# Sigmoid attention and SwiGLU on one core: two more quads transposed by DMA, halves of a tile written by two engines, a later first visit, last stores by rows

## The chip, the core and the metric

The kernel runs on one core of a Trainium2 chip. The core has engines that run side by side, each with its own queue of instructions: TensorE (PE, matmuls; PEld is its weight load), VectorE (DVE), ScalarE (ACT), GpSimd (POOL) and SyncE (SP). Data moves between the chip's memory (HBM), the on-chip SBUF and, on the core, the matmul accumulator PSUM. Transfers are issued from the queues of SP, ACT and POOL and carried out by the core's 16 DMA engines. The metric is the device time of one execution in microseconds (us); lower is better.

## The reference

```python
scores = q @ k.transpose(0, 1, 3, 2) / sqrt(64) - log(448)     # 8 batches, 12 heads, 448 x 64
attn_out = sigmoid(scores) @ v                                 # no softmax: a plain sigmoid
x = attn_out.transpose(0, 2, 1, 3).reshape(3584, 768)
g = x @ w_gate                                                 # 768 x 1536
out = (g * sigmoid(g) * (x @ w_val)) @ w_out                   # 1536 x 768, float32
```

## The kernel before

The attention works in **quads**: four heads of one batch, three quads per batch, 24 in all (quad n belongs to batch n // 3). One quad goes through these steps:

- `load` (L129) brings q and k as float32 into a staging tile `st` (448 KB each); `load_v` (L134) brings v as float16.
- `cast` (L139) makes a bf16 tile `c16` of it, on VectorE for the first quads, on GpSimd (L145) for the later ones.
- The bf16 tile is transposed into `T` (pool `qkT`, four buffers for q and four for k). `trans_pe` (L159) does it on TensorE: 14 matmuls against an identity (L167) into PSUM and two copies out of it on VectorE (L175). `trans_dma` (L150) does it by two DMA transposes issued on SyncE (L153), one for q and one for k.
- `qk_tile` (L185) makes the scores of one seventh of the keys (4 matmuls, L191), `sig_tile` (L200) takes the sigmoid on ScalarE (L202), and `pv` (L205) multiplies with v once all seven are there (28 matmuls, L214). The result is copied out of PSUM into two tiles `xT` of 128 partitions, each in two halves of 64 (L228 on VectorE). For quad 2, with `two=True`, ScalarE copies the second halves (L226).

The feed-forward part uses `xT` as its right-hand side. `ffn1` (L246) computes one of 12 feature tiles f of one batch: 12 matmuls (L239), a sigmoid on ScalarE (L253) and two multiplications on VectorE (L255, L259) that write `hT`. `ffn2` (L265) computes one of 7 output tiles for a pair of batches: 24 matmuls (L273), an eviction in two halves on VectorE (L307) and two stores of 64 rows each (L318). For the very last tile the second half is evicted by ScalarE (L293, 192 columns) and VectorE (L300, 192 columns), and each half is stored by two transfers, one from SyncE and one from ScalarE (L315).

All PSUM users take turns on a ring of four buffers `D0` to `D3`, two banks each (`Banked`, L75). The framework tracks which instruction reads and writes which tile and adds the waits; `add_to_no_dep_group` and `declare_no_dep` take a wait away where the program knows that there is no conflict.

The order of the work is written out by hand. The prologue (L361 to L434) handles quads 0 to 2 and the first two feature tiles of batch 0. Then a loop (L465) walks over `units`, the feature and output tiles with planned times of 2.26 and 3.9 us. Into it it inserts **visits** (L339): each quad from 3 on has two, the first with four of its score tiles, the second with three. A visit is due when the planned time `tcur` has reached its `vtime` (L340 to L348). For the quads of batch 1 (3, 4, 5) these due times are spread evenly between `2 * FU1` and `FIRST`.

The tables `begin` (L449 to L459) say what GpSimd and SyncE are given after a visit: `ready(n)` (L441) casts quad n and, for n >= `NPE`, issues its DMA transposes; `fetch(n)` (L436) loads quad n; `w_load` (L113) loads a quarter of w_gate, w_val or w_out (576 KB as float16). `NPE = 2 * NJ = 6`, so quads 4 and 5 are transposed on TensorE: `post` (L476, L486) calls `trans_pe` one unit behind the second visit of the quad before. GpSimd's queue is in program order: a fetch stands behind the casts that were issued ahead of it, and a cast waits for its load to land.

Of the kernel before, what the change touches and what calls it, by code (L numbers as in the profile page):

```python
# [9 lines left out]
FP32 = mybir.dt.float32  # L10
# [3 lines left out]
MULT = mybir.AluOpType.mult  # L14
# [3 lines left out]
def kernel(  # L18
# [10 lines left out]
    nc = tc.nc  # L29
    ctx.enter_context(tc.manual_schedule())  # L30

    B, H, S, D = q.shape
    DM = H * D
    DFF = moe_w_gate.shape[1]
    C = S // D
    NJ = H // 4
# [5 lines left out]
    HREC = 1.0 / HSC  # L42
# [86 lines left out]
    def load(n, which, eng=None):  # L129
        st = stg.tile([128, 2, S], FP32, tag="stg", name=f"st{which}_{n}")  # L130
        (eng or nc.sync).dma_start(out=st, in_=src_of(n, which))  # L131
        qkv_st[(n, which)] = st

    def load_v(n):  # L134
        t = v16p.tile([128, 2, S], FP16, tag="v16", name=f"v16_{n}")
        nc.gpsimd.dma_start(out=t, in_=src_of(n, 2))  # L136
        v16[n] = t

    def cast(n, which, eng, lo=0, hi=C):  # L139
        st = qkv_st[(n, which)]  # L140
        if hi == C:
            qkv_st.pop((n, which))
        t = c16.tile([128, hi - lo, 2, D], BF16, tag="c16" if hi - lo == C else f"c16_{lo}", name=f"c16_{which}_{n}")
        q16[(n, which, lo)] = t
        eng.tensor_copy(  # L145
            out=t.rearrange("p c h d -> p h c d"),
            in_=st.rearrange("p h (c d) -> p h c d", c=C)[:, :, lo:hi, :],
        )

    def trans_dma(n, which):  # L150
        t = q16.pop((n, which, 0))
        d = qkT.tile([128, C, 128], BF16, tag=f"T{which}", name=f"T{which}_{n}")
        nc.sync.dma_start_transpose(out=d, in_=t.rearrange("p c h d -> p (c h d)"))  # L153
        for c in range(C):
            qT[(n, which, c)] = d[:, c]
        if which == 0:
            qT[(n, 0)] = d

    def trans_pe(n, parts=((0, 0, C), (1, 0, C))):  # L159

        D2 = Banked()
        ps = D2.t.bitcast(BF16).rearrange("p w (c i) -> p w c i", c=8)
        for i, (which, lo, hi) in enumerate(parts):
            t = q16.pop((n, which, lo))
            for c in range(hi - lo):
                D2.write(
                    nc.tensor.transpose(  # L167
                        out=ps[:, i, c, :], in_=t[:, c].rearrange("p h d -> p (h d)"), identity=idn
                    ),
                    i,  # L170
                )
        for i, (which, lo, hi) in enumerate(parts):
            tag = f"T{which}" if hi - lo == C else f"T{which}_{lo}"
            d = qkT.tile([128, hi - lo, 128], BF16, tag=tag, bufs=None if hi - lo == C else 1, name=f"T{which}_{n}_{lo}")
            D2.read(nc.vector.tensor_copy(out=d, in_=ps[:, i, :hi - lo, :]), i)  # L175
            for c in range(lo, hi):
                qT[(n, which, c)] = d[:, c - lo]
            if which == 0:
                qT[(n, 0)] = d
# [25 lines left out]
    def pv(n, two=False):  # L205
        b, j = divmod(n, NJ)
        P = Banked().t
        vt = v16.pop(n)
        for c in range(C):
            pt = pts.pop((n, c))  # L210
            for h2 in range(2):
                for w in range(2):
                    r = slice(w * 64, w * 64 + 64)
                    nc.tensor.matmul(  # L214
                        out=P[h2 * 64:(h2 + 1) * 64, w, :S],
                        lhsT=vt[r, h2, c * D:(c + 1) * D],
                        rhs=pt[r, h2, :],
                        start=(c == 0),
                        stop=(c == C - 1),
                    )  # L220
        for h2 in range(2):
            x = xtp.tile([128, S], FP16, tag="xT", name=f"xT_{b}_{2 * j + h2}")
            for w in range(2):
                o, i = x[w * 64:(w + 1) * 64, :], P[h2 * 64:(h2 + 1) * 64, w, :S]
                if two and w == 1:
                    nc.scalar.copy(out=o, in_=i)  # L226
                else:
                    nc.vector.tensor_copy(out=o, in_=i)  # L228
            xT[(b, 2 * j + h2)] = x


# [33 lines left out]
    def ffn2(pb, m):  # L265
        hw = DM // 2
        osb = osp.tile([128, DM], FP32, tag="osb", name="osb")
        D = Banked("o")
        for half in range(2):
            for f in range(NF):  # L270
                h = hT[(pb, f)].rearrange("p b s -> p (b s)")
                D.write(
                    nc.tensor.matmul(  # L273
                        out=D.t[:, half, :hw],
                        lhsT=h[:, m * 128:(m + 1) * 128],
                        rhs=wo16[f // FW][:, f % FW, half * hw:(half + 1) * hw],
                        start=(f == 0),
                        stop=(f == NF - 1),
                    ),
                    half,  # L280
                )
        last = pb == B // 2 - 1
        dsts = []
        for i in range(2):
            bb, c = divmod(2 * m + i, C)
            bb += 2 * pb
            dsts.append(out[bb * S:(bb + 1) * S, :].rearrange("(p c) n -> c p n", c=C)[c])
        for half in range(2):
            hs = slice(half * hw, (half + 1) * hw)
            if last and m == C - 1 and half == 1:  # L290
                qw = hw // 2
                D.read(
                    nc.scalar.activation(  # L293
                        out=osb[:, hw:hw + qw], in_=D.t[:, 1, :qw],
                        func=mybir.ActivationFunctionType.Copy, scale=HREC,
                    ),
                    1,
                )
                D.read(
                    nc.vector.tensor_scalar(  # L300
                        out=osb[:, hw + qw:], in0=D.t[:, 1, qw:hw], scalar1=HREC, scalar2=None, op0=MULT
                    ),
                    1,
                )
            else:
                D.read(
                    nc.vector.tensor_scalar(  # L307
                        out=osb[:, hs], in0=D.t[:, half, :hw], scalar1=HREC, scalar2=None, op0=MULT
                    ),
                    half,  # L310
                )
            if last and m == C - 1:
                for i in range(2):
                    eng = nc.sync if i == 0 else nc.scalar
                    eng.dma_start(out=dsts[i][:, hs], in_=osb[i * 64:(i + 1) * 64, hs])  # L315
        if not (last and m == C - 1):
            for i in range(2):
                (nc.sync if last else nc.gpsimd).dma_start(out=dsts[i], in_=osb[i * 64:(i + 1) * 64, :])  # L318


    FU1, FU2 = 2.26, 3.9
# [18 lines left out]
    vtime = []  # L340
    for grp in visits:
        n, c = grp[0]
        b, j = divmod(n, NJ)
        frac = (j * C + c) / (NJ * C)
        if b == 1:
            vtime.append(2 * FU1 + frac * (FIRST - 2 * FU1))
        else:
            vtime.append(FIRST + 1.0 + (b - 2 + frac) * PER)  # L348

# [5 lines left out]
            for n, c, sc in scs:  # L355
                sig_tile(n, c, sc)

    NPE = 2 * NJ


    V, G = nc.vector, nc.gpsimd  # L361
# [7 lines left out]
    cast(0, 1, V, 0, 2)  # L369
    trans_pe(0, ((0, 0, C), (1, 0, 2)))  # L370
    cast(0, 1, V, 2, C)

    def chunk(n, c):
        sig_tile(n, c, qk_tile(n, c))
# [39 lines left out]
    pv(1)  # L414
    chunk(2, 3)
    trans_pe(3)
    cast(4, 0, G)
    cast(4, 1, G)
    w_load("v", 2)
    load_v(5)  # L420
    w_load("g", 3)
# [11 lines left out]
        ffn1_mm(Df, 0, f, range(NP - 2, NP))  # L433
        ffn1_gate(Df, 0, f)  # L434

    def fetch(n):  # L436
        load(n, 0, G)
        load(n, 1, G)
        load_v(n)

    def ready(n):  # L441
        cast(n, 0, G)
        cast(n, 1, G)
        if n >= NPE:
            trans_dma(n, 0)
            trans_dma(n, 1)


    begin = {(n, i): [] for n in range(NJ, NQ) for i in range(2)}  # L449
    begin[(4, 0)] += [lambda: ready(5), lambda: fetch(6)]  # L450
# [10 lines left out]

    tcur = 2 * FU1
    vi = 0
    pend, post = [], []
    for dur, fn, args in units:  # L465
        while vi < len(visits) and tcur >= vtime[vi]:
            group = visits[vi]
            vi += 1
            pvs, pend = pend, []
            attn_step(group, pvs)  # L470
            n, c = group[-1]
            for act in begin[(n, int(c == C - 1))]:
                act()
            if c == C - 1:
                pend.append(n)
                if n + 1 < NPE:  # L476
                    post.append(n + 1)
        if pend and (
            fn is ffn1 and args[1] == 0 and (args[0], NP - 1) not in xT
            or vi == len(visits) and tcur >= vtime[-1] + 4.0  # L480
        ):
            for n in pend:
                pv(n)
            pend = []
        fn(*args)
        while post:  # L486
            trans_pe(post.pop())
        tcur += dur


# [28 lines left out]
```

## Time and profile before

| what | value |
|---|---|
| median of 11 runs | 442.28 us (439.11 to 443.74) |
| profiled execution | 440.32 us, of which the span of its instructions is 438.5 us |
| granted TensorE clock in it, mean | 0.992 |
| TensorE transposes L167 | 14 matmuls in 0.94 us per quad |
| ffn1 matmuls L239 | 1152 of about 353 ns |
| ffn2 matmuls L273 | 672 of 326 ns |
| loads issued by GpSimd, median to landing | q 5.2, k 8.7, v 9.5, w_gate 14.5, w_val 15.0, w_out 17.2 us |
| DMA transposes, 36 of them, median to landing | 6.1 us |

The page's busy time per engine is a share of the whole span. Its DMA row cuts the span into 40 slices of about 11 us, each digit being the busy tenths of the 16 DMA engines. q0 is the queue of transfers that GpSimd issues, q1 that of SyncE. "To landing" is the time from issue to the last byte, and so holds the time that a transfer waits behind others.

### The profile page before, as it was taken

The numbers are of one execution on the slowest core, as the hardware profiler recorded it, in microseconds if no ns is written. First come the engines' busy times: TensorE is split into PE (matmuls) and PEld (weight loads), VectorE is DVE, ScalarE is ACT, GpSimd is POOL, SyncE is SP. The second block draws the span as 40 slices with busy tenths as digits, with TensorE's granted clock in tenths as the row PEclk, the third lists the DMA queues.
The fourth block names the chain that finished last, engine by engine and source line by source line (L and its number), as shares of the span: only waits on it lengthen the run. The fifth ranks groups of instructions, "written<-read, shape, count | busy, mean of one in ns | idle before, by whom it ended". The sixth has DMA issues, their size and how long they took to land.

```text
span 438.5 us, 7904 instructions
## 1 busy us (share of the span) xinstructions
PE 417.3 (95%) x3261; PEld 219.5 (50%) x3261; DVE 220.2 (50%) x364; ACT 207.7 (47%) x269; POOL 116.1 (26%) x166
## 2 busy tenths in 40 slices
PE   6788779999999999999999999999999999999995
PEld 3434345445555445445555545444555545555563
DVE  3644646465344457556434456647524356555331
ACT  4967557546433555645533655745623452222000
POOL 4464434042255546000245534400012200000000
PEclk8999989999999999999999999999999999999999
DMA  8999999999598998600198999820022400000144
GB/s 303 237 269 205 244 165 187 148 114 183 116 136 196 253 216 157 134 1 1 29 137 192 219 150 216 197 43 1 0 73 73 100 9 1 1 1 1 42 103 108
DMA packets 57796, 54.38 MB, mean 124 GB/s; under 512 B 35680, under 2 KB 52448, under 8 KB 57760
## 3 DMA queue, kind: packets, MB, share of 16 engines
q0 software_dynamic: 20896, 39.20, 43.4%
q1 hardware_dynamic: 36432, 14.03, 20.9%
q10 hardware_dynamic: 432, 0.66, 0.4%
q8 instruction: 25, 0.41, 0.4%
q14 instruction: 11, 0.09, 0.1%
HBM read 47.19 MB, written 11.01 MB: 133 GB/s over the span
## 4 chain that ended last, share of the span: by engine, by line
PE 82%; ACT 8%; DVE 4%; issue 3%; DMA 1%; DVEq 0%; ACTq 0%
PE ps_D L239 48%; PE ps_D L273 25%; ACT pt L202 7%; PE ps_D L191 6%; PE ps_D L214 3%; DVE xT L228 1%; DVE hT L259 1%; DMA st<-in_q_dram 1%; DVE T L175 1%; DVE t L255 1%; ACT s L253 1%; DVE c L145 0%; ACT xT L226 0%; PE ps_D L167 0%; DVE osb L300 0%
## 5 line engine op out<-in xcount | busy, mean ns | idle before, releaser
L202 ACT ACTIVATE pt<-ps_D,sb_t 128x896 f16<-128x896 f32 x168 | 156.0, 1008 | 96.6 <-PE ps_D L191 96.6
L239 PE MATMUL ps_D<-xT,wg 128*128 128x448 f16 x576 | 125.3, 353 | 2.5 <-ACT xT L226 0.8
L239 PE MATMUL ps_D<-xT,wv 128*128 128x448 f16 x576 | 125.0, 352 | 0.0
L273 PE MATMUL ps_D<-wo,hT 128*128 128x384 f16 x672 | 111.7, 326 | 0.8 <-ACT pt L202 0.4
L255 DVE TENSOR_TENSOR t<-ps_D,s 128x448 f16<-128x448 f32 x96 | 59.8, 623 | 89.5 <-ACT s L253 88.0
L253 ACT ACTIVATE s<-ps_D 128x448 f16<-128x448 f32 x96 | 52.5, 547 | 98.2 <-PE ps_D L239 98.2
L273 PEld LDWEIGHTS <-hT 128*128 128x128 f16 x672 | 65.2, 98 | 47.1 <-issue 4.6
L239 PEld LDWEIGHTS <-wg 128*128 128x128 f16 x576 | 54.7, 98 | 59.7 <-issue 12.0
L239 PEld LDWEIGHTS <-wv 128*128 128x128 f16 x576 | 56.4, 98 | 53.5 <-issue 1.0
L228 DVE CAST xT<-ps_D 64x448 f16<-64x448 f32 x94 | 58.5, 622 | 33.7 <-PE ps_D L214 32.2
L307 DVE TENSOR_SCALAR osb<-ps_D 128x384 f32<-128x384 f32 x55 | 30.6, 557 | 71.8 <-PE ps_D L273 65.8
L259 DVE SCALAR_TENSOR_TENSOR hT<-ps_D,t 128x448 f16<-128x448 f32 x96 | 60.0, 625 | 10.4 <-DVE t L255 0.5
L145 POOL CAST c<-st 128x896 bf16<-128x896 f32 x41 | 37.9, 934 | 84.5 <-issue 43.9
L318 POOL DMA_DIRECT2D out_dram<-osb x42 | 22.3, 536 | 137.3 <-DVE osb L307 137.3
L191 PE MATMUL ps_D<-T,T 64*64 64x448 bf16 x672 | 47.1, 363 | 10.0 <-DVE T L175 6.7
L214 PE MATMUL ps_D<-pt,v 64*64 64x448 f16 x672 | 37.3, 359 | 1.0 <-ACT pt L202 1.0
L191 PEld LDWEIGHTS <-T 64*64 64x64 bf16 x672 | 16.2, 107 | 32.7 <-issue 19.5
L214 PEld LDWEIGHTS <-v 64*64 64x64 f16 x672 | 20.3, 110 | 14.2 <-issue 3.3
L136 POOL DMA_DIRECT2D v<-in_v_dram x24 | 17.7, 739 | 0.1
L131 POOL DMA_DIRECT2D st<-in_k_dram x20 | 14.7, 734 | 3.0 <-issue 3.0
L131 POOL DMA_DIRECT2D st<-in_q_dram x20 | 14.6, 732 | 0.6 <-DMA v<-in_v_dram 0.6
L293 ACT ACTIVATE osb<-ps_D 128x192 f32<-128x192 f32 x1 | 0.3, 330 | 27.9 <-PE ps_D L273 27.9
(21 smaller groups left out, 43.7 us busy)
## 6 DMA issues: line engine op xcount, KB each, us to landing
st<-in_q_dram POOLq DMA_DIRECT2D x20, 448.0 KB, 5.2
st<-in_k_dram POOLq DMA_DIRECT2D x20, 448.0 KB, 8.7
out_dram<-osb POOLq DMA_DIRECT2D x42, 192.0 KB, 3.1
v<-in_v_dram POOLq DMA_DIRECT2D x24, 224.0 KB, 9.5
wg<-in_moe_w_gate_dram POOLq DMA_DIRECT2D x4, 576.0 KB, 14.5
wv<-in_moe_w_val_dram POOLq DMA_DIRECT2D x4, 576.0 KB, 15.0
wo<-in_moe_w_out_dram POOLq DMA_DIRECT2D x4, 576.0 KB, 17.2
out_dram<-osb SPq DMA_DIRECT2D x12, 192.0 KB, 2.7
```

The costliest lines, as they stand in the source:

```text
L131: (eng or nc.sync).dma_start(out=st, in_=src_of(n, which))
L145: eng.tensor_copy(out=t.rearrange("p c h d -> p h c d"), in_=st.rearrange("p h (c d) -> p h c d", c=C)[:, :, lo:hi, :],)
L191: nc.tensor.matmul(out=sc[w * 64:(w + 1) * 64, h2, :S], lhsT=kt[r, w * 64:(w + 1) * 64], rhs=qt[r, :, w * 64:(w + 1) * 64], start=True, st ...
L202: nc.scalar.activation(out=pt, in_=sc[:, :, :S], func=SIGM, bias=sb_t, scale=qkscale)
L214: nc.tensor.matmul(out=P[h2 * 64:(h2 + 1) * 64, w, :S], lhsT=vt[r, h2, c * D:(c + 1) * D], rhs=pt[r, h2, :], start=(c == 0), stop=(c == C ...
L228: nc.vector.tensor_copy(out=o, in_=i)
L239: nc.tensor.matmul(out=D.t[:, i, :S], lhsT=w16[f // FW][:, pr, cs], rhs=xT[(b, pr)], start=(pr == 0), stop=(pr == NP - 1),),
L253: D.read(nc.scalar.activation(out=s16, in_=D.t[:, 0, :S], func=SIGM), 0)
L255: D.read(nc.vector.tensor_tensor(out=t1, in0=D.t[:, 0, :S], in1=s16, op=MULT), 0)
L259: nc.vector.scalar_tensor_tensor(out=hT[(b // 2, f)][:, b % 2, :], in0=D.t[:, 1, :S], scalar=HSC, in1=t1, op0=MULT, op1=MULT),
L273: nc.tensor.matmul(out=D.t[:, half, :hw], lhsT=h[:, m * 128:(m + 1) * 128], rhs=wo16[f // FW][:, f % FW, half * hw:(half + 1) * hw], start ...
L307: nc.vector.tensor_scalar(out=osb[:, hs], in0=D.t[:, half, :hw], scalar1=HREC, scalar2=None, op0=MULT),
```

## The change

It has four parts. `NPE` becomes `NJ + 1 = 4`, so that `ready(4)` and `ready(5)` issue DMA transposes on SyncE (for quad 4 in the prologue, directly behind its casts; for quad 5 behind its casts, after the first visit of quad 4) and the two calls of `trans_pe` in the loop are gone. The due times of batch 1's visits start at `3 * FU1`, so that one more feature tile (f = 2) comes ahead of the first. In `pv(2, two=True)` the wait between the two halves of one `xT` tile is taken away. In the last output tile the second half is evicted by rows: ScalarE takes the upper 64 rows, VectorE the lower, into tiles of their own, and each is stored from its own queue; the first half is stored by two transfers of SyncE.

```diff
                 if two and w == 1:
-                    nc.scalar.copy(out=o, in_=i)
+                    cp = nc.scalar.copy(out=o, in_=i)
+                    tc.declare_no_dep(cp.ins, group=f"half{n}_{h2}", reason="other partitions")
                 else:
-                    nc.vector.tensor_copy(out=o, in_=i)
+                    cp = nc.vector.tensor_copy(out=o, in_=i)
+                    if two:
+                        tc.add_to_no_dep_group(f"half{n}_{h2}", cp.ins)
...
-            if last and m == C - 1 and half == 1:
-                qw = hw // 2
-                D.read(
-                    nc.scalar.activation(
-                        out=osb[:, hw:hw + qw], in_=D.t[:, 1, :qw],
...
+            if end and half == 1:
+
+                for i in range(2):
+                    r = slice(i * 64, i * 64 + 64)
+                    oe = osp.tile([128, hw], FP32, tag=f"oe{i}", bufs=1, name=f"oe{i}")
+                    if i == 0:
+                        ev = nc.scalar.activation(
+                            out=oe[r], in_=D.t[r, 1, :hw], func=mybir.ActivationFunctionType.Copy, scale=HREC
+                        )
+                    else:
+                        ev = nc.vector.tensor_scalar(
+                            out=oe[r], in0=D.t[r, 1, :hw], scalar1=HREC, scalar2=None, op0=MULT
+                        )
+                    D.read(ev, 1)
+                    (nc.scalar if i == 0 else nc.sync).dma_start(out=dsts[i][:, hs], in_=oe[r])
...
-            if last and m == C - 1:
-                for i in range(2):
-                    eng = nc.sync if i == 0 else nc.scalar
-                    eng.dma_start(out=dsts[i][:, hs], in_=osb[i * 64:(i + 1) * 64, hs])
+                if end:
+                    for i in range(2):
+                        nc.sync.dma_start(out=dsts[i][:, hs], in_=osb[i * 64:(i + 1) * 64, hs])
...
         if b == 1:
-            vtime.append(2 * FU1 + frac * (FIRST - 2 * FU1))
+            vtime.append(3 * FU1 + frac * (FIRST - 3 * FU1))
...
-    NPE = 2 * NJ
+    NPE = NJ + 1
...
     trans_pe(3)
-    cast(4, 0, G)
-    cast(4, 1, G)
+    ready(4)
     w_load("v", 2)
...
             if c == C - 1:
                 pend.append(n)
-                if n + 1 < NPE:
-                    post.append(n + 1)
...
         fn(*args)
-        while post:
-            trans_pe(post.pop())
         tcur += dur
```

More of the change, by code (lines that the diff above doesn't have):

```diff
@@ L267, in ffn2 @@
         osb = osp.tile([128, DM], FP32, tag="osb", name="osb")
+        dsts = []
+        for i in range(2):
+            bb, c = divmod(2 * m + i, C)
+            bb += 2 * pb
+            dsts.append(out[bb * S:(bb + 1) * S, :].rearrange("(p c) n -> c p n", c=C)[c])
         D = Banked("o")
@@ L282, in ffn2 @@
         last = pb == B // 2 - 1
-        dsts = []
-        for i in range(2):
-            bb, c = divmod(2 * m + i, C)
-            bb += 2 * pb
-            dsts.append(out[bb * S:(bb + 1) * S, :].rearrange("(p c) n -> c p n", c=C)[c])
+        end = last and m == C - 1
         for half in range(2):
             hs = slice(half * hw, (half + 1) * hw)
-            if last and m == C - 1 and half == 1:
-                qw = hw // 2
-                D.read(
-                    nc.scalar.activation(
-                        out=osb[:, hw:hw + qw], in_=D.t[:, 1, :qw],
[L295 to L304, printed above, removed]
+            if end and half == 1:
[12 more added lines that the diff above has]
+                    (nc.scalar if i == 0 else nc.sync).dma_start(out=dsts[i][:, hs], in_=oe[r])
             else:
@@ L311, in ffn2 @@
                 )
-            if last and m == C - 1:
-                for i in range(2):
-                    eng = nc.sync if i == 0 else nc.scalar
-                    eng.dma_start(out=dsts[i][:, hs], in_=osb[i * 64:(i + 1) * 64, hs])
-        if not (last and m == C - 1):
+                if end:
+                    for i in range(2):
+                        nc.sync.dma_start(out=dsts[i][:, hs], in_=osb[i * 64:(i + 1) * 64, hs])
+        if not end:
             for i in range(2):
@@ L371, with fetch, ready @@
     cast(0, 1, V, 2, C)
+    def fetch(n):
+        load(n, 0, G)
+        load(n, 1, G)
+        load_v(n)
+    def ready(n):
+        cast(n, 0, G)
+        cast(n, 1, G)
+        if n >= NPE:
+            trans_dma(n, 0)
+            trans_dma(n, 1)
     def chunk(n, c):
@@ L434 @@
         ffn1_gate(Df, 0, f)
[L436 to L446, printed above, removed]
     begin = {(n, i): [] for n in range(NJ, NQ) for i in range(2)}
@@ L463 @@
     vi = 0
-    pend, post = [], []
+    pend = []
     for dur, fn, args in units:
```

## The prediction

> **What bounds the kernel now.** I read the page's first two parts, then the waits of PE, then the DMA queues by stretch, then single landings. TensorE is busy 95% of the span, so outside a few waits the end is the sum of its work. The DMA row says something else about the first 110 us (ten slices of 11 us): 8 or 9 tenths in every one.
>
> ```profile
> PE 417.3 (95%) x3261; PEld 219.5 (50%) x3261; DVE 220.2 (50%) x364; ACT 207.7 (47%) x269; POOL 116.1 (26%) x166
> DMA  8999999999598998600198999820022400000144
> ```
>
> TensorE's own waits from 24 to 75 us are all of them what this change is aimed at (line waited for, us in total, times, longest):
>
> ```profile
> PE ps_D L191 <- DVE T L175: 4.5, 2, 2.3
> PE ps_D L191 <- DVE hT L259: 1.3, 2, 0.7
> PE ps_D L191 <- DVE xT L228: 1.1, 1, 1.1
> PE ps_D L239 <- ACT xT L226: 0.8, 1, 0.8
> ```
>
> No DMA stands in that list: every load and transpose lands in time. The question is by how much. First the queues, 27 to 51 us, in which GpSimd's loads run alone, and 54.3 to 107.8 us, in which SyncE's transposes run beside them (packets, MB, share):
>
> ```profile
> q0 software_dynamic: 5464, 5.80, 124.3%
> ...
> q0 software_dynamic: 3199, 6.44, 69.9%
> q1 hardware_dynamic: 7607, 1.88, 49.6%
> ```
>
> In 24 us q0 alone moves 5.80 MB; beside the transposes 6.44 MB takes 53.5 us. Both queues had work waiting all that time, so a transpose takes time from the loads. Then three landings: the key transpose of quad 6, the last quarter of w_out, and two transposes in a quiet stretch.
>
> ```profile
> L153 SPq DMA_TRANSPOSE T<-c x1: 1235/1235/1235, 51.8 to 51.8; - x1
> DMA to landing us min/median/max: 12.5/12.5/12.5
> ...
> L116 POOL DMA_DIRECT2D wo<-in_moe_w_out_dram x1: 794/794/794, 90.8 to 90.8; - x1
> DMA to landing us min/median/max: 17.0/17.0/17.0
> ...
> L153 SPq DMA_TRANSPOSE T<-c x2: 1227/1229/1231, 292.2 to 293.5; - x2
> DMA to landing us min/median/max: 2.9/3.0/3.0
> ```
>
> Quad 6's keys land at 51.8 + 12.5 = 64.3; its first QK matmul starts at 71.09: 6.8 us to spare. Quad 7's land at 65.6 + 13.8 = 79.4 for a use at 85.72: 6.3 us. The last w_out quarter lands at 90.8 + 17.0 = 107.8. The first ffn2 tile starts at 109.71 and comes to features 9 to 11 after nine matmuls of 24 in 3.90 us, at 111.2: **3.4 us to spare**, the least I find.
>
> **The change, part by part.**
>
> *Transposes of quads 4 and 5 off TensorE.* Removed are 2 x 14 matmuls of L167 (0.94 us a set, at 43.08 and 56.28) and four L175 copies (0.615 us each), and with them the wait for those copies, 2.26 us before the QK at 46.29 and again at 59.49. That is 2 x (0.94 + 2.26) = 6.4 us of TensorE's path.
>
> *First visit of batch 1 behind tile f = 2.* Today QK of quad 3 waits 0.58 + 0.69 = 1.3 us for the gates (hT) of f = 0 and 1. With a whole tile (2.27 us) in front, the gates are done: 1.2 us gained, since the fourth score tile now waits for the gate of f = 2, whose last step ends about 1 us behind its matmuls while three QK tiles take 1.0 us.
>
> *Halves written at once.* Today the four copies of pv(2) run one after the other, 29.07 to 31.47. In the built program ScalarE's first copy waits for PE alone, while VectorE's second still waits for ScalarE's first: two pairs side by side, 2 x 0.63 = 1.26 us instead of 2.4: 1.15 us gained, all on the chain (the L226 and L228 waits above).
>
> So TensorE could reach quad 6's QK 6.4 + 1.2 + 1.15 = **8.8 us** earlier, at 62.3.
>
> *What is added.* Four DMA transposes on SyncE's queue, two behind the casts of quad 4 (POOL, 24.72 to 26.5), two behind those of quad 5 (33.3 to 35.4). SyncE issues nothing between 4.9 and 50.36 us, so no instruction stands behind them there but later transposes. Their cost is in the DMA engines. Loads alone land 1.15 us apart for a q or k quad, 1.05 us for v, 2.9 us for a weight slice (for example 34.3 k, 35.3 v, 38.2 and 41.2 w, from issue and landing). From 54.3 (w_out 0: 38.5 + 15.8) to 73.1 (w_out 1: 55.8 + 17.3) there landed four q/k, two v and one weight slice: 4 x 1.15 + 2 x 1.05 + 2.9 = 9.6 us of loads in 18.8 us. The other 9.2 us go with 2713 packets of q1; one transpose is 928 (q1 from 121.2 to 124.2, which holds one), so 2.9 of them: **3.15 us each**. By the long stretch, to 107.8: loads 8 x 1.15 + 4 x 1.05 + 3 x 2.9 = 22.1 of 53.5 us, 31.4 us over 8.2 transposes: 3.8 each. From below: in the quiet pair one follows the other at the issue's 1.23 us. Between 27 and 51 us q0 is backed up (loads land 12 to 16 us behind their issue), which is the busy case; I take 3.15, the stretch next to it. Four make D = 12.6 us (4.9 to 15.3).
>
> A page bears on this from the other side. The Trainium skill, "DMA: Bandwidth & Descriptors", section "Issuing engines are not separate DMA queues", says that DMAs of all issuing engines run on the same 16 engines and interleave, which is what the two queue rows show. The page's fit (section "Anatomy of one DMA", for GpSimd's path) would price the 229 KB of a transpose at an estimated 0.53 us beyond the fixed part, D = 2.1 us, and a result near 441; its section "Specifications" also says that transfers under 512 B miss line rate, and the transposes' packets are such. The measured rows decide, and they are six times dearer.
>
> *Where D goes.* GpSimd issues in order, and each fetch stands behind the casts of data that landed before it; the SW queue is never empty from 16 to 108 us. So everything that lands after T5 lands D later: w_val slice 2 (41.2 us, used by f = 6 at 52.1, 10.9 us to spare) just about when it is used, quad 6's keys at 64.3 + 12.6 = 76.9, quad 7's at 92.0, the last w_out quarter at 120.4. TensorE's 8.8 us are then all waited away: QK of quad 6 starts 12.6 - 6.8 = 5.8 us later than now, quad 7's 6.3, and ffn2 of the first pair **12.6 - 3.4 = 9.2 us** later. Behind 109 us GpSimd's fetches stand behind stores, which wait for TensorE, and what lands there has 10 us and more to spare (quad 9's keys: 105.5 for 118.24), so nothing is added and nothing is got back. What TensorE saved before 60 us is worth nothing then; it would be worth 8.8 us only with this queue's cover gone.
>
> *Last stores.* Today ScalarE 0.33 us and VectorE 0.36 us one after the other, 434.18 to 434.90, then two stores. After it each has 64 rows x 384, priced by their rows of like width: about 0.47 us (547 ns at 448 wide) and 0.557 us (L307). In the built program VectorE still waits for ScalarE, since both read the same PSUM buffer: 434.18 + 0.47 + 0.03 + 0.56 = 435.24, and SyncE's store starts 0.35 us later, ScalarE's 0.25 earlier. The later one sets the end: +0.35 (-0.2 if they run together). The first half's two stores, now both on SyncE at 432.8, take about 0.5 us of issue each and are out before.
>
> **Sum.** On the profiled execution (440.32 us, span 438.5): 440.3 + 9.2 + 0.35 = 449.9. It stands 2.0 us under the median of 442.28, which I carry over: 451.8, said as **451.5**.
>
> **Rivals.**
>
> *Hidden transposes (faster).* They slip into gaps of the weight loads: w_out 0 landed 2.9 us behind v6 although quad 6's first transpose ran in the same time. It decides if the four cost the load queue under 0.8 us together. Against it, the 9.2 us above. Even then the last w_out quarter lands at 107.8, so that of 8.8 us only 3.4 stay: 442.28 - 3.4 + 0.35 = 439.2. Chance 0.10.
>
> *Cheap transposes (no change).* At 1.23 us each D = 4.9 and 442.28 + 4.9 - 3.4 + 0.35 = 444.1. For it: packets of T alone are short. Against it: that stretch had no loads. Chance 0.14.
>
> *Dearer ones.* Beside loads a transpose takes 53.5 / 8.2 = 6.5 us, and T5 may be late for quad 5 too; at 3.8 us and above D is 15.3 or more, 454.5 and up. Chance 0.16.
>
> Forecast, 449 to 454: chance 0.60. A measurement of this kernel tells about 0.5%, 2.2 us, from no change. Faster 0.10, same 0.14, slower 0.76. The range 441 to 457 leaves out most of the first rival and the far end of the last.
>
> **What would show it.** L167 with 28 fewer matmuls and no L175 wait at 46 and 59; T landings from about 26 us on; loads from 30 to 60 us landing later; TensorE waiting for DMA at quad 6's QK and at the first ffn2 tile. I am wrong if q0's landings up to 54 us stay where they are, or if w_out's last quarter lands before 112.

## The result, and the profile after

| | before | after |
|---|---|---|
| median | 441.28 us (47 runs) | 448.03 us (12 runs) |
| ratio | | 1.0145, 95% interval 1.0118 to 1.0172 |
| profiled execution, its span | 440.32, 438.5 us | 446.78, 445.0 us |
| mean granted clock | 0.992 | 0.976 |

The granted clock is the share of full speed that TensorE's clock was given. A ratio counts only the runs within 1.5% of their kernel's fastest one, while a median counts all of them, which matters most in run 4 below, where six of twelve fall out.

The change makes the kernel about 6.5 us slower. The first lines of the page after, engines and DMA:

```profile
PE 419.8 (94%) x3233; PEld 218.7 (49%) x3233; DVE 217.8 (49%) x360; ACT 208.3 (47%) x269; POOL 116.4 (26%) x166
...
DMA  8999999999989999810077999921022310000144
```

TensorE has 28 matmuls fewer and is busy 2.5 us longer. Its waits from 20 to 130 us (line waited for, us in total, times, longest) have changed hands:

```profile
PE ps_D L191 <- DMA T<-c: 8.7, 2, 5.9
PE ps_D L281 <- DMA wo<-in_moe_w_out_dram: 2.1, 1, 2.1
PE ps_D L191 <- DVE xT L229: 1.1, 1, 1.1
PE ps_D L191 <- DVE T L175: 0.6, 1, 0.6
```

The 4.5 us of waits for VectorE's copies of T at quads 4 and 5 are gone (the 0.6 us left lie ahead of 24 us and are in both kernels), and DMA, which TensorE did not wait for in this stretch before, holds it up for 10.8. The chain of waits (start, us, what) runs through the loads now, where it ran through TensorE, ScalarE and VectorE before:

```profile
39.29 19.53 DMA st<-in_k_dram
...
62.80 12.97 DMA st<-in_k_dram
...
77.49 16.94 DMA st<-in_k_dram
...
97.82 18.16 DMA wo<-in_moe_w_out_dram
115.98 0.04 issue
116.02 4.28 PE ps_D L281 x15
```

Quad 6's keys, quad 8's, quad 9's, then the last quarter of w_out; the tenth matmul of the first ffn2 tile starts 0.04 us behind its landing. From there on no transfer stands in the chain. The DMA queues over the same loads, from 26 us to the landing of the first w_out quarter, show what held them up: first the kernel before (26 to 54.3 us), then the kernel after (26 to 62.8 us); the columns are packets, MB and share of the 16 engines.

```profile
q0 software_dynamic: 5967, 6.34, 116.8%
q1 hardware_dynamic: 732, 0.19, 7.6%
```

```profile
q0 software_dynamic: 5964, 6.34, 96.9%
q1 hardware_dynamic: 4434, 1.10, 29.0%
```

The same 6.34 MB of loads take 36.8 us instead of 28.3. What was added is 3702 packets on q1, 4.0 transposes of 928: **2.1 us of the loads' time for each**. Where both queues have work, their packets go one for one, as the rows of the kernel after from 38 to 48 us show; how much of the 2.1 us this alone explains is open.

```profile
q0 software_dynamic: 1887, 1.45, 91.4%
q1 hardware_dynamic: 1892, 0.46, 35.8%
```

The last line of the account is a clock. Stretches from the table by window (us, busy us of PE, PEld, DVE, ACT and POOL with counts, then granted clock, DMA share, GB/s), of the kernel after: its longest wait and its wait at ffn2, each with the stretch behind it.

```profile
66.50:72.30 5.80, 0.00 (x0) 0.00 (x0) 0.78 (x2) 0.00 (x0) 0.93 (x1) 0.70 1.17 152
72.30:76.00 3.70, 3.65 (x44) 1.75 (x44) 0.07 (x1) 1.91 (x2) 1.99 (x3) 0.54 1.18 283
...
114.00:116.00 2.00, 0.00 (x0) 0.00 (x0) 0.00 (x0) 0.00 (x0) 0.00 (x0) 1.00 1.26 126
116.00:120.30 4.30, 4.28 (x19) 1.97 (x22) 0.56 (x1) 0.00 (x0) 0.00 (x0) 0.60 1.27 168
```

Behind the wait at 114 us the granted clock is 0.60 for 4.3 us: fifteen matmuls take 4.28 us that take 2.45 at the spacing of the chain before (24 in 3.90 us). So this wait costs more than it lasts.

**The sum.** The first ffn2 tile on TensorE, before, then after:

```profile
109.55 4.06 PE L273 MATMUL ps_D<-wo,hT 128*128 128x384 f16 x24
...
112.32 1.63 PE L281 MATMUL ps_D<-wo,hT 128*128 128x384 f16 x9
116.02 4.28 PE L281 MATMUL ps_D<-wo,hT 128*128 128x384 f16 x15 [2.07 <-DMA wo<-in_moe_w_out_dram]
```

The last w_out quarter lands at 115.98 instead of 107.81, 8.2 us later. The tenth ffn2 matmul, which uses it, stood at 111.01 (109.55 and nine of 24 in 3.90 us) and stands at 116.02: 5.0 us. From there to the last matmul's end it is 324.8 us instead of 323.1: 1.7 us, about what the low clock costs (4.28 - 2.45 = 1.8). From the last matmul to the end of the span it is 4.2 us instead of 4.4: -0.2. Together 6.5 us, which is 445.0 - 438.5.

### The profile page after: what moved, and what is told of

It reads as the page before. It is cut to its first block, busy times and chain, and to the rows that moved or that the text cites. A ratio compares the mean times of both kernels' runs of the same rounds, so it can differ in the third digit from the quotient of the medians.

```text
span 445.0 us, 7849 instructions
## 1 busy us (share of the span) xinstructions
PE 419.8 (94%) x3233; PEld 218.7 (49%) x3233; DVE 217.8 (49%) x360; ACT 208.3 (47%) x269; POOL 116.4 (26%) x166
## 4 chain that ended last, share of the span: by engine, by line
PE 68%; DMA 21%; ACT 5%; DVE 2%; issue 2%; POOL 1%; ACTq 0%; DVEq 0%; POOLq 0%
PE ps_D L242 37%; PE ps_D L281 25%; DMA st<-in_k_dram 15%; PE ps_D L191 4%; DMA wo<-in_moe_w_out_dram 4%; ACT pt L202 4%; DMA st<-in_q_dram 2%; PE ps_D L214 2%; PE ps_D L167 1%; POOL c L145 1%; DVE T L175 1%; DVE hT L262 0%; DVE t L258 0%; DVE xT L229 0%; DVE c L145 0%
## 5 line engine op out<-in xcount | busy, mean ns | idle before, releaser
L281 PE MATMUL ps_D<-wo,hT 128*128 128x384 f16 x672 | 113.5, 329 | 2.9 <-DMA wo<-in_moe_w_out_dram 2.1
L242 PEld LDWEIGHTS <-wg 128*128 128x128 f16 x576 | 54.5, 98 | 59.8 <-issue 12.3
L191 PE MATMUL ps_D<-T,T 64*64 64x448 bf16 x672 | 48.3, 374 | 13.0 <-DMA T<-c 8.7
L214 PE MATMUL ps_D<-pt,v 64*64 64x448 f16 x672 | 38.5, 368 | 0.8 <-ACT pt L202 0.8
## 6 DMA issues: line engine op xcount, KB each, us to landing
st<-in_q_dram POOLq DMA_DIRECT2D x20, 448.0 KB, 5.0
st<-in_k_dram POOLq DMA_DIRECT2D x20, 448.0 KB, 10.5
```

The source lines that it names most:

```text
L191: nc.tensor.matmul(out=sc[w * 64:(w + 1) * 64, h2, :S], lhsT=kt[r, w * 64:(w + 1) * 64], rhs=qt[r, :, w * 64:(w + 1) * 64], start=True, st ...
L214: nc.tensor.matmul(out=P[h2 * 64:(h2 + 1) * 64, w, :S], lhsT=vt[r, h2, c * D:(c + 1) * D], rhs=pt[r, h2, :], start=(c == 0), stop=(c == C ...
L242: nc.tensor.matmul(out=D.t[:, i, :S], lhsT=w16[f // FW][:, pr, cs], rhs=xT[(b, pr)], start=(pr == 0), stop=(pr == NP - 1),),
L281: nc.tensor.matmul(out=D.t[:, half, :hw], lhsT=h[:, m * 128:(m + 1) * 128], rhs=wo16[f // FW][:, f % FW, half * hw:(half + 1) * hw], start ...
```

## The experiments

Two theories at the start. **Load queue:** the four extra transposes take DMA time from the loads behind them, and the loss is set where a late load meets its first user. **Late tiles:** TensorE loses only what it waits for the transposed tiles at QK. A third, that the other three edits cost the time, had to be shut out. Ratios are against the kernel before, run beside each.

### 1. The rest of the change without its transposes

```diff
-    NPE = NJ + 1
+    NPE = 2 * NJ
...
+                if n + 1 < NPE:
+                    post.append(n + 1)
...
+        while post:
+            trans_pe(post.pop())
```

> The changed kernel with quads 4 and 5 transposed on TensorE again; the three other edits stay. Load-queue theory (the four DMA transposes hold up GpSimd's loads by some 8 us, and that sets the loss): no load moves, TensorE gains 1.2 us from the later visit, 1.15 us from the halves and 0.2 us at the end, and the 3.4 us to spare at the last w_out quarter still cover it: 2.5 us faster than before, ratio about 0.994. Rival (the loss comes from the other edits): slower than before, 1.01 or more. Rival (late tiles: TensorE only waits for the transposed tiles themselves): the same as the first.

Measured 0.9965 (0.9937 to 0.9994), median 439.18 us. The other edits are a gain and not the loss. Of the 2.5 us hoped for some 1.5 came: in the profiled run the last w_out quarter landed at 110.6 us, and TensorE, being early, waited 0.4 us for it.

### 2. The transposes alone

```diff
-    NPE = 2 * NJ
+    NPE = NJ + 1
...
     cast(4, 1, G)
+    trans_dma(4, 0)
+    trans_dma(4, 1)
```

> The kernel before with nothing changed but that quads 4 and 5 go through DMA transposes. Load-queue theory: loads from 36 us on land 8 us later as in the changed kernel, and the first ffn2 tile waits for the last w_out quarter: 1.014 to 1.016, as the whole change. Rival (other edits cost): 0.985 to 0.99, since TensorE's 6.4 us are then a gain. Rival (late tiles): QK of quad 6 waits, but the gain of 6.4 us covers it: 1.00 to 1.01.

Measured 1.0174 (1.0132 to 1.0216), median 448.49 us: the whole loss, within its interval of the full change. The 6.4 us that it takes off TensorE appear nowhere in the time. Its two DMA waits:

```profile
PE ps_D L191 <- DMA T<-c: 10.3, 3, 9.6
PE ps_D L273 <- DMA wo<-in_moe_w_out_dram: 1.9, 1, 1.9
```

The shares differ from the full change: TensorE comes to its first ffn2 tile 4.9 us late (114.48), by the wait at quad 6's QK and a low clock behind that, then waits for w_out, and behind that wait the clock is not low (15 matmuls in 2.60 us).

### 3. The transposes for nobody

TensorE does all that it did; quads 4 and 5 are transposed by DMA a second time, into tiles that nothing reads.

```diff
+    def trans_extra(n):
+        for which in range(2):
+            t = q16[(n, which, 0)]
+            d = qkT.tile([128, C, 128], BF16, tag=f"X{which}", bufs=1, name=f"X{which}_{n}")
+            nc.sync.dma_start_transpose(out=d, in_=t.rearrange("p c h d -> p (c h d)"))
...
     cast(4, 1, G)
+    trans_extra(4)
...
-    begin[(4, 0)] += [lambda: ready(5), lambda: fetch(6)]
+    begin[(4, 0)] += [lambda: ready(5), lambda: trans_extra(5), lambda: fetch(6)]
```

> The kernel before, with TensorE still transposing quads 4 and 5, and four DMA transposes of the same casts into tiles that nobody reads. Load-queue theory: the loads land 8 us later all the same; QK of quad 6 waits about 1 us, the first ffn2 tile for the last w_out quarter, 8.2 - 3.4 = 4.8 us later, and up to 2 us more go on a TensorE clock that is low behind the waits: 1.011 to 1.016. Rival (late tiles) and rival (other edits): nobody waits for the extra tiles and nothing else is changed: 1.00.

Measured 1.0059 (1.0025 to 1.0094), median 443.44 us (440.87 to 447.91). Slower, though no instruction waits for these tiles: the late-tile theory cannot give that. In size it is half of what I expected. The profiled run is among its longer ones (445.58 us); it has, from 26 to 62.3 us, the queues of the changed kernel, and one new wait (here L279 is the ffn2 matmul):

```profile
q0 software_dynamic: 5964, 6.34, 97.0%
q1 hardware_dynamic: 4377, 1.09, 28.3%
```

```profile
PE ps_D L279 <- DMA wo<-in_moe_w_out_dram: 3.6, 1, 3.6
```

The first w_out quarter lands 8.0 us late (8.5 in the changed kernel), the last one 7.0 us late (114.8), and the wait is for that load: TensorE came to that tile at 109.58, as before, and then stood. GpSimd's buffers are not what the extra transposes hold up here: its cast of quad 6 waits 14.1 us for the load of that quad. The spread of the runs, 7 us, is wider than the effect. A reading is that the landings between 60 and 108 us differ from run to run, and that what is left of the 8 us at the last quarter decides the run; with one trace of this kernel that is not shown.

### 4. One quad instead of two

Quad 4 back on TensorE, quad 5 by DMA, the other edits kept.

```diff
-    NPE = NJ + 1
+    NPE = 2 * NJ - 1
```

> The changed kernel with quad 4 back on TensorE and quad 5 alone by DMA: two extra transposes instead of four. Load-queue theory: the loads land about 4 us later, 0.6 us over the 3.4 us to spare at the last w_out quarter, plus up to 1 us of low clock, less 0.2 us at the end: 1.001 to 1.003. Rival (late tiles): half of the 8.7 us of waits at QK, against half of the gain: 1.007. Rival (other edits): 1.01 as before.

Measured 0.9929 (0.9886 to 0.9972), but median 441.98 us (1.003 of the kernel before) with runs from 435.30 to 445.12: the spread says more than the ratio. The expectation lies inside the spread and is not confirmed by it. The profiled run, of 444.37 us, is one in which the load came late. Queues from 26 to 58.3 us, and its largest wait:

```profile
q0 software_dynamic: 5967, 6.34, 106.0%
q1 hardware_dynamic: 2517, 0.63, 19.2%
```

```profile
PE ps_D L281 <- DMA wo<-in_moe_w_out_dram: 6.7, 1, 6.7
```

1785 more packets (1.9 transposes) for 4.0 us more: 2.1 us each again. TensorE reached ffn2 4.0 us *earlier* than before (105.56) and then stood for 6.7 us.

### 5. and 6. The last w_out quarter one quad earlier

If that load sets the end, moving it from quad 7's second visit to quad 6's (two visits earlier), ahead of quad 10's loads, takes the wait away. In run 5 this is done to the changed kernel, in run 6 to the kernel before, as a control.

```diff
-        begin[(4 + i, 1)].append(lambda i=i: w_load("o", i))
+        begin[(min(4 + i, 6), 1)].append(lambda i=i: w_load("o", i))
```

> The changed kernel, with the last w_out quarter issued one visit earlier, together with the third and ahead of quad 10's loads. Theory (the last w_out quarter is the load that sets the end; the waits at QK of quads 5 and 6 cost only what TensorE had gained): TensorE reaches the first ffn2 tile 2.8 us later than before, as in the changed kernel, and then waits no more: the 2.1 us of wait and some 1.7 us of low clock behind it are gone: 1.004 to 1.008 instead of 1.0145. Rival (the loss comes from the late transposed tiles at QK of quads 5 and 6, 8.7 us of waits): no change from the changed kernel, 1.013 and more.

> The kernel before with the same move of the last w_out quarter, as a control. Theory: nothing waits for it before, so 0.999 to 1.001. Rival (the move is a gain by itself): 0.995 or less.

Measured 1.0073 (1.0046 to 1.0101), median 444.09 us, for the changed kernel, and 1.0008 (0.9986 to 1.003) for the control. Moving one load takes half of the loss away, and is worth nothing measurable where nobody waits for it. The waits of the changed kernel with the early load, from 20 to 130 us:

```profile
PE ps_D L191 <- DMA T<-c: 9.1, 2, 6.5
PE ps_D L191 <- DVE xT L229: 1.7, 2, 1.1
```

The waits at QK are still there, w_out's is gone. So the waits at QK, of quads 5 and 6, are what eats up TensorE's gain (and about 3 us more), and w_out's wait with its low clock is the other half.

### 7. Transposes on TensorE, put better

The wait for L175 can be hidden without DMA: the same 14 matmuls ahead of the feature tile, so that the copies run under it. With the other edits and the early load of run 5.

```diff
-    NPE = NJ + 1
+    NPE = 2 * NJ
...
+                if n + 1 < NPE:
+                    post.append(n + 1)
...
+        while post:
+            trans_pe(post.pop())
         fn(*args)
```

> Transposes of quads 4 and 5 on TensorE, but put ahead of the feature tile instead of behind it, so that the copies out of PSUM run under its 2.27 us; the later visit, the halves and the stores as in the changed kernel; the last w_out quarter early as in the run above. Theory: the two waits of 2.3 us for L175 go, and some 1.3 us of low clock behind one of them; TensorE reaches the first ffn2 tile about 6.9 us before the kernel before, no load is held up, and QK of quad 7 may wait 0.6 us for its keys: 0.982 to 0.988. Rival (the loads of q and k bound this stretch anyway): 0.995 or more.

Measured **0.985** (0.9825 to 0.9874), median 434.37 us: the fastest of all. The windows of both, 40 to 63 us of this kernel and the second of the two waits before, show the hole closed and the clock held:

```profile
40.00:63.00 23.00, 22.76 (x228) 11.71 (x226) 14.98 (x25) 18.57 (x24) 7.85 (x10) 1.00 1.20 193
```

```profile
57.20:59.50 2.30, 0.04 (x5) 0.02 (x4) 2.13 (x4) 0.00 (x0) 0.93 (x1) 1.00 1.37 80
59.50:63.00 3.50, 3.50 (x40) 1.86 (x44) 0.00 (x0) 1.91 (x2) 0.00 (x0) 0.52 0.84 114
```

TensorE is busy 22.76 of 23 us at full clock; the kernel before stood 2.3 us at 57.2 and then ran 3.5 us at a clock of 0.52.

### 8. What a transpose costs beside other loads

My price of 3.15 us came from the stretch from 54.3 us on. Here four extra transposes of quads 7 and 8 fall into that stretch (tiles that nothing reads; `trans_extra` as in run 3, with the cast kept for it).

```diff
             trans_dma(n, 1)
+        if n in (7, 8):
+            trans_extra(n)
```

> The kernel before with four extra DMA transposes of the casts of quads 7 and 8, each pair behind its own transposes, into tiles that nobody reads: the same four, but beside loads of q and k instead of weights and v. If a transpose costs the loads the same everywhere (2.05 us as the two kernels' traces show between 26 and 55 us), the last w_out quarter lands 8.2 us later, TensorE waits about 5 us: 1.011 to 1.016. If it costs 3.15 us beside q and k loads, as the prediction had it: 12.6 us later, 1.020 to 1.026.

Measured 0.9998 (0.9978 to 1.0018), median 441.12 us: **neither expectation held.** The extra four cost the time nothing. First w_out quarter to last, the kernel before (54.3 to 107.8 us, shown in the prediction) moved 6.44 MB on q0 beside 7607 packets on q1 in 53.5 us. This kernel, 54.5 to 105.7 us:

```profile
q1 hardware_dynamic: 9812, 2.42, 46.6%
...
q0 software_dynamic: 3197, 6.43, 71.2%
```

2205 packets more on q1 (2.4 transposes), the same loads, and 51.2 us. So the loads' time in this stretch is no simple count of the transposes beside them. It is not a clean price either, since most of the extra packets found q0 nearly empty: GpSimd's cast of quad 9 waited 19.45 us for an extra transpose to free its buffer (14.29 us for a load before), from 86 to 94 us q1 moved 3992 packets (1489 before) and q0 78, and the last w_out quarter, issued 3.3 us later than before, landed 11.6 us behind its issue instead of 17.0. What the extra ones delay is the transposes behind them on SyncE's queue: quad 9's keys land at 116.7 instead of 105.5, still ahead of their use at 121.4.

### 9. and 10. The parts of the fastest run, and one quad by DMA with room for it

Run 9 is run 1 with the early load, run 10 is run 4 with it.

> The changed kernel with quads 4 and 5 transposed on TensorE behind the feature tile, as before, and the last w_out quarter early: the first of the eight runs plus the move of the load. It tells what the order of the transposes was worth in the fastest run. Theory: TensorE's 2.35 us from the visit and the halves and 0.2 us at the end: 0.993 to 0.996; the two waits of 2.3 us for L175 and the low clock are still there. Rival (the early w_out load is what made that run fast): 0.985 to 0.988.

> Quad 5 alone by DMA (two extra transposes), the three other edits, and the last w_out quarter early. Theory (what a DMA transpose costs depends on the room that the loads behind it have): TensorE no longer waits for w_out, reaches the first ffn2 tile about 4 us before the kernel before, QK of quad 6 waits for its keys at most 1 us: 0.988 to 0.993, where the same kernel with the late load ran from 0.987 to 1.01. Rival (the transposes cost the loads too much in any case): 0.998 or more.

Measured 0.9939 (0.9912 to 0.9966), median 438.06 us, and 0.9886 (0.9853 to 0.9919), median 435.76 us. Of run 7's 1.5%, 0.6% are the other edits with the load early; the order of the transposes is the rest. And a DMA transpose in place of TensorE's is a gain after all where the loads behind it have room: quad 5's pair, with no wait for w_out left, is worth half a per cent (run 10 against run 9).

## Why the prediction was right

The forecast, 451.5 us by way of the load queue with the last w_out quarter as the place that decides, was right in sign, mechanism and place. Its size was 9.55 us against 6.5, by one term that was too large and one that was missing; these two pull opposite ways, so that the total is nearer than its largest term, which is luck. The measured 448.0 us lies inside 441 to 457 and 1 us under the band of 449 to 454; about 1 us of the difference to 451.5 is the base, 442.28 from 11 runs and 441.28 from 47. Neither sign of being wrong came: the loads of quad 6 landed 8.5 us later, and the last w_out quarter at 116.

- *TensorE's gain.* Forecast 8.8 us by quad 6's QK, of which nothing would be left. TensorE finished its last tile ahead of that QK at 66.5 us, against 71.1 before: 4.6 us earlier with 2.8 us of wait for quad 5's tiles inside, so 7.4 without that wait. The low clock behind quad 5's QK is no part of the difference, since both kernels have it (28 PV matmuls in 2.84 us before, 2.81 after). Of the 1.4 us missing, 0.4 stood ahead of the change (the PV of quad 1 starts at 21.36 instead of 20.96), and a wait of 0.45 us for the gate of f = 2 was left, where 0.1 was allowed. Then TensorE stood for 5.9. Run 2 shows that none of it reaches the end. For quad 5's tiles themselves being late the sum had no term; it was only a remark beside a rival. That wait lay inside the later ones and did not count.
- *Price of a transpose: the mis-sized term.* "3.15 us each" measured 2.1 (run 3: 2.0, run 4: 2.1), so D was 8.2 and not 12.6. I had put the whole slowness of the loads from 54.3 us on down to the transposes beside them, on the reading that both queues had work all that time. They had not: from 60 to 65 us before, q1 moved only 156 packets, and q0 still no more than 0.84 MB in 5 us, 0.17 MB per us, where it had moved 5.80 MB in 24 us alone, 0.24. And the same working gives no fixed price: 3.8 us before, but (51.2 - 22.1) / 10.6 = 2.7 in run 8's stretch. The 2.1 us hold between 26 and 62 us, where q1 was idle before. What does set the loads' pace behind 54 us I have not found out.
- *D carried on unchanged.* "Lands D later" held: 8.5 us for quad 6 and the first w_out quarter, 8.0 and 7.5 for the next two, 8.2 for the last. It is not exact from run to run: run 3's profile went from 8.0 to 7.0, run 4's from 4.0 to 6.1.
- *The place.* 12.6 - 3.4 became 8.2 - 3.2 = 5.0 (the first ffn2 tile starts at 109.55 and not at 109.71, so 3.2 us were to spare). Runs 5 and 6 show that this place sets the last half of the loss. The other half is quad 6's QK: it came 1.26 us later (72.35 against 71.09, forecast 5.8) and cost 1.5 us of low clock, so that TensorE was 2.8 us late at its first ffn2 tile, about what run 5 was left with (444.09 against 441.34).
- *The missing term.* 1.7 us of low clock behind the wait at ffn2, which the sum put at nothing. The trace before had it to be read, 0.52 behind the wait at 59.5; I took the wait's length for its price.
- *Last stores.* Forecast +0.35; the end took 0.2 us less, on one profile, which is no more than such ends differ between runs: 4.1 to 4.4 us in the traces of either form of the last stores. VectorE does wait for ScalarE (440.88 + 0.48, then 441.40), as the built program said.
- *Halves and first visit.* The four copies ran in pairs, 29.41 to 30.75 instead of 29.07 to 31.47. Runs 1 and 9 put these two and the stores together at 0.4 to 0.6%.

The rival of hidden transposes is refuted by runs 2 and 3; what spoke for it, the first transpose that ran beside a w_out load without delaying it, is one transfer, and why it cost nothing is not shown. The rival of cheap ones (1.23 us) is refuted by the queue rows.

One rule of the Trainium skill fits what was seen: "DMA: Bandwidth & Descriptors", section "Issuing engines are not separate DMA queues", says that SyncE's and GpSimd's transfers share 16 engines. The two queue rows above fit that: the same 6.34 MB in 28.3 and 36.8 us. The estimate that the prediction drew from the page's fit for GpSimd's path, 0.53 us for a transpose's bytes, is a quarter of the 2.1 measured.

## What to carry to other kernels

Work taken off a busy engine and given to a queue can be paid for by what is queued behind it, so look for the landing with the least time to spare downstream, not for the wait that the edit removes: here 3.2 us at a load 60 us later; with that one moved, the next place still cost half. Price a transfer only from a stretch in which it alone differs; a backed-up stretch charges its other delays to it. And try the cheap reordering on the engine first: here, moving 14 matmuls ahead of a tile that hides their copies was worth more than moving them to DMA (run 7 against runs 5 and 10).

## What the hardware showed that was not expected

- A wait of TensorE of 2.1 to 2.3 us can be enough to bring the granted clock to 0.5 or 0.6 for the next 3.5 to 4.3 us (0.60 behind 114 us after, 0.52 behind 57.2 before). Not always: behind the equal wait that ended at 46.3 us before, the clock stayed at 1.00 for the next 3.7 us, and behind run 5's 2.6 us at quad 5's QK 28 PV matmuls took 1.49 us, full pace. The Trainium skill, "TensorE: Matmul & The Clock Gate", section "Why this matters for your kernels", advises against gaps of more than about 3 us; here shorter ones did it.
- A DMA transpose has no fixed price. Beside loads on an otherwise idle q1 it cost them 2.1 us; four more behind 54 us left the last w_out landing no later (105.7 against 107.8), and the keys of quad 9 landed 11 us later.
